# A new order table for a one-core adaLN block: attention tiles spread, w_sp blocks moved behind the stages' own transposes, x added by TensorE in five tiles

## The chip, the cores and the metric

The kernel runs on one core of one Trainium2 chip. The metric is the device time of one execution in microseconds (us), from the first to the last instruction and what lies around them. The kernel before has a median of 252.75 us over three runs (252.35, 252.75 and 254.44). A change of 1% is 2.5 us.

## What is computed

A block of a transformer with S = 2048 rows x, D = 448, 16 heads of width 28 (all in bfloat16). The reference, cut to what matters:

```
h = layernorm(x) * (1 + ca) + sa          # ca, sa, ... from silu(c) @ w_mod
q, k, v = h @ wqkv                        # 16 heads of 28
phi(t)  = [softmax(t @ w_phi), softmax(-t @ w_phi)]
o = (phi(q) @ (phi(k)^T v)) / (phi(q) . sum phi(k))
x = x + ga * (o @ wo)
h = layernorm(x) * (1 + cb) + sb
z = gelu(h @ w_in);  z1, z2 = halves of 896
g = w_sp @ layernorm(z2) + b_sp           # w_sp is 2048 x 2048: over the rows
out = x + gb * ((z1 * g) @ w_out)
```

## The kernel before, in words

The work is cut into 16 row tiles of 128 (numbers 0 to 15). All steps are emitted by one loop in `fast_path`, which reads a table of words, `ORDER`: `kM:12@A1` calls step `kM` for tile 12 with PSUM slot A1, `nA:8/V` calls `nA` for tile 8 on VectorE. An engine executes its instructions in the order of the words, so the table is the schedule. The letters behind a slash are engines: V is VectorE (DVE), S is ScalarE (ACT), G is GpSimd (POOL), Y is SyncE's DMA queue (SP). The slots behind @ are PSUM buffers: A0, A1, A2 of two banks, B0, B1 of one bank. A step that takes a slot waits until the readers of the slot's last contents are done.

The stages, by the words and the lines of the kernel before:

- **The ramp**: loads, weights folded with w_phi and the modulation, the first four tiles transposed by TensorE.
- **Keys and values**: `l1a` normalises a row tile on POOL (L824), `T1:a,b` has the SP queue transpose tiles a to b-1 into hT (L829), `kM` and `vM` are four matmuls each (L847, L855), `kE` and `kF` the exponentials on ACT (L850), `kS`, `kR`, `kP` the softmax sums and products (L861, L865, L868), `kA` adds a tile into phi(k)^T v (L878). `qM:n` makes features of 512 rows of q (L902, eight matmuls), `qE` and `qF` its two exponentials on ACT (L907).
- **Attention**: for each tile `nM` (L930, eight small matmuls into a slot A), `nX` (ACT, L938), `nC` and `nS` (DVE, L941 to L947; `nS` serves two tiles), `nT` (DVE, L950, the last reader of the slot), `nA` (DVE or POOL, L956), `T2` (SP transposes the result, L829), then `wM` or `wN`: four matmuls with wo (L966). In `wN` a fifth matmul with the identity adds x on TensorE (L964) and ACT copies the sum out with `wR:i/S` (L971). With `wM`, DVE adds x in `wR:i/V` (L973). Seven tiles go by `wN`: 0, 1, 2, 3, 4, 10, 11.
- **The second layernorm and the wide layer**: `wQ` (square and sum), `l2R`, `l2r`, `l2a` normalise tile i again, `T3:a,b` transposes it into hT over SP (L1004), `zM` is eight matmuls for z2 (L1010, slot A), `zG` its gelu on ACT (L1014), `zQ`, `zR`, `zW`, `zN` its layernorm. `yM:st,fc` is four matmuls for z1 (L1039), which need the four tiles 4st to 4st+3, `yG` its gelu on ACT (L1042). `SHw` and `SCw` fold the modulation into w_in (L740, L753 to L757), `csB`, `ccB` are its columns (L721).
- **The mixing by w_sp**: `W:t,u` (L1047) has the SP queue load and transpose one of 32 blocks (128 x 1024) of w_sp. `W:0` goes to a buffer of its own (f_wsp), `W:1` and `W:2` into the two halves of f_Eq, once `nM` has read tiles 0 to 7 or 8 to 15, `W:3` into hT, once all `zM` and `yM` are done. `gM` (L1106) and `P` (L1085) are the matmuls over w_sp, in a scheme with seven products for eight; `tT`, `sS` make their sums, `d` and `x` (L1094, L1101) read out; `oM` (L1120), `oE`, `oD` make and store the output.

SP's queue holds, besides the loads, all of T1, T2, T3 and W in the order of the words: one that waits holds up all behind it. The word `dm:9,3` issues nine small matmuls on zeros into a free corner of tile 3's slot (L935); they compute nothing.

Of the kernel before, what the change touches and what calls it, by code (L numbers as in the profile page):

```python
# [476 lines left out]
CB = HP * DH  # L477
TCHF = 512
SUM_MAX = 4.0e12

# [747 lines left out]
```

## Time and profile before

| What | Value |
|---|---|
| median of three runs | 252.75 us |
| the profiled execution | 253.16 us |
| its span, first to last instruction | 251.3 us |
| PE busy | 241.7 us (96%), 1550 matmuls |
| DVE, ACT, POOL busy | 186.2, 105.9, 119.1 us |
| DMA, 68208 packets | 25.23 MB |
| chain that ended last | PE 77%, DVE 11%, DMA 4%, POOL 3% |

Stage by stage, from the stretches of the trace: keys and values lie at about 21.5 to 54.1 us of the span, attention with the start of the wide layer at 54.1 to 105, the rest of the wide layer to 139.4, the mixing to the end. A row of the time line reads: start in us, length in us, engine, line, operation, out<-in, shapes, count, and in brackets how long the engine stood idle before it and what ended that. Rows of matmuls overlap: a row's length holds the time in which its last result drains, so the distance of two starts tells what a group costs, not its length.

### The profile page before, as it was taken

The numbers are of one execution on the slowest core, as the hardware profiler recorded it, in microseconds if no ns is written. First come the engines' busy times: TensorE is split into PE (matmuls) and PEld (weight loads), VectorE is DVE, ScalarE is ACT, GpSimd is POOL, SyncE is SP. The second block draws the span as 40 slices with busy tenths as digits, with TensorE's granted clock in tenths as the row PEclk, the third lists the DMA queues.
The fourth block names the chain that finished last, engine by engine and source line by source line (L and its number), as shares of the span: only waits on it lengthen the run. The fifth ranks groups of instructions, "written<-read, shape, count | busy, mean of one in ns | idle before, by whom it ended". The sixth has DMA issues, their size and how long they took to land.

```text
span 251.3 us, 4227 instructions
## 1 busy us (share of the span) xinstructions
PE 241.7 (96%) x1550; PEld 127.1 (51%) x1550; DVE 186.2 (74%) x378; ACT 105.9 (42%) x219; POOL 119.1 (47%) x161
## 2 busy tenths in 40 slices
PE   8999998999989799999999999999999999999993
PEld 5865555576546454444444444444444444444451
DVE  4799999777999968874548999599976436644552
ACT  2498977735879658896897300000000000000000
POOL 3749997503568663486834064101119511034530
PEclk9999999999999999999999999999999999999999
DMA  7987569951588849789691977000001000101022
GB/s 181 275 231 173 97 144 200 233 141 21 103 164 113 158 85 183 122 146 221 121 179 28 172 133 77 0 0 0 3 0 37 0 3 1 55 0 37 21 92 68
DMA packets 68208, 25.23 MB, mean 100 GB/s; under 512 B 58129, under 2 KB 67602, under 8 KB 68178
## 3 DMA queue, kind: packets, MB, share of 16 engines
q1 hardware_dynamic: 64848, 20.78, 42.5%
q10 hardware_dynamic: 3330, 4.09, 5.9%
q8 instruction: 14, 0.23, 0.4%
q14 instruction: 16, 0.13, 0.2%
HBM read 8.87 MB, written 1.84 MB: 43 GB/s over the span
## 4 chain that ended last, share of the span: by engine, by line
PE 77%; DVE 11%; DMA 4%; POOL 3%; issue 2%; ACT 1%; POOLq 0%; DVEq 0%
PE g_ps L1085 29%; PE z_ps L1039 10%; PE z_ps L1010 9%; PE o_ps L1120 8%; PE g_ps L1106 5%; DMA f_hT<-f_xpad 4%; PE x_ps L966 3%; PE warm_ps L686 3%; DVE f_st L813 3%; PE q_ps L902 2%; PE v_ps L855 2%; DVE f_ar L950 2%; PE kvacc L878 2%; DVE f_ksum L861 2%; PE num L930 2%
## 5 line engine op out<-in xcount | busy, mean ns | idle before, releaser
L1094 DVE TENSOR_TENSOR f_zb<-g_ps,f_zb 128x512 f32<-128x512 f32 (+1 forms) x31 | 20.3, 669 | 17.5 <-PE g_ps L1085 17.1
L1085 PEld LDWEIGHTS <-f_z2n 128*128 128x128 bf16 x192 | 18.8, 98 | 22.5
L1101 POOL TENSOR_TENSOR f_z1T<-f_zb,f_z1T 128x512 bf16<-128x512 f32 (+1 forms) x11 | 11.9, 1102 | 35.0 <-DVE f_zb L1094 35.0
L1039 PE MATMUL z_ps<-f_hT,f_ar 112*128 112x512 bf16 x112 | 26.3, 379 | 1.3 <-DMA f_hT<-f_xpad 1.3
L1010 PE MATMUL z_ps<-f_ar,f_hT 112*128 112x448 bf16 (+1 forms) x128 | 26.5, 352 | 0.0
L1120 PE MATMUL o_ps<-f_wout,f_z1T 128*128 128x448 bf16 x112 | 22.5, 352 | 0.0
L1085 PE MATMUL g_ps<-f_ar 128*128 128x512 bf16 x96 | 22.2, 379 | 0.0
L1042 ACT ACTIVATE f_z1T<-z_ps,f_zb 128x512 bf16<-128x512 f32 x28 | 18.4, 683 | 6.7 <-PE z_ps L1039 6.7
L1101 POOL TENSOR_TENSOR f_z1T<-f_Sx,f_z1T 128x512 bf16<-128x512 f32 x6 | 7.1, 1182 | 27.2 <-DVE f_Sx L1094 27.2
L907 ACT ACTIVATE f_Eq<-q_ps 112x1024 bf16<-112x1024 f32 x16 | 16.1, 1036 | 6.5 <-PE q_ps L902 6.5
L1010 PEld LDWEIGHTS <-f_hT 112*128 112x128 bf16 (+1 forms) x128 | 12.2, 97 | 11.7 <-DMA f_hT<-f_xpad 0.3
L1039 PEld LDWEIGHTS <-f_ar 112*128 112x128 bf16 x112 | 10.9, 97 | 14.2 <-issue 1.8
L861 DVE TENSOR_REDUCE f_ksum<-f_E 128x32 f32<-128x896 bf16 x16 | 16.7, 1056 | 1.4 <-ACT f_E L850 1.4
L950 DVE TENSOR_TENSOR f_ar<-num,f_w 128x896 bf16<-128x896 f32 x16 | 16.9, 1084 | 0.4
L1014 ACT ACTIVATE f_zb<-z_ps 128x896 bf16<-128x896 f32 x16 | 14.6, 915 | 5.6 <-PE z_ps L1010 4.4
L850 ACT ACTIVATE f_E<-k_ps 128x448 bf16<-128x448 f32 x32 | 16.0, 556 | 1.7 <-PE k_ps L847 1.6
L1085 PE MATMUL g_ps<-f_Eq,f_z2n 128*128 128x512 bf16 x72 | 16.7, 379 | 0.0
L1120 PEld LDWEIGHTS <-f_z1T 128*128 128x128 bf16 x112 | 11.0, 98 | 10.7
L1123 DVE TENSOR_TENSOR f_xpad<-o_ps,f_x 128x448 bf16<-128x448 f32 x16 | 9.9, 621 | 8.0 <-PE o_ps L1120 7.9
L847 PE MATMUL k_ps<-f_Wk,f_hT 113*128 113x448 bf16 (+1 forms) x64 | 14.6, 352 | 0.8 <-DMA f_hT<-f_xpad 0.8
L902 PE MATMUL q_ps<-f_hT,f_Wq 113*128 113x512 bf16 (+1 forms) x64 | 15.0, 379 | 0.1
L1085 PEld LDWEIGHTS <-f_ar 128*128 128x128 bf16 x96 | 9.4, 98 | 11.2
(207 smaller groups left out, 483.1 us busy)
## 6 DMA issues: line engine op xcount, KB each, us to landing
out_dram<-f_xpad SPq DMA_DIRECT2D x16, 112.0 KB, 1.7
f_ar<-in_B_w_in_dram ACTq DMA_DIRECT2D x2, 784.0 KB, 5.3
f_wm<-in_w_mod_dram SPq DMA_DIRECT2D x3, 406.0 KB, 5.8
f_x<-in_A_x_dram SPq DMA_DIRECT2D x2, 448.0 KB, 8.7
f_wmg<-in_w_mod_dram ACTq DMA_DIRECT2D x2, 392.0 KB, 4.2
f_wout<-in_B_w_out_dram SPq DMA_DIRECT2D x1, 784.0 KB, 5.3
f_bsp<-in_B_b_sp_dram SPq DMA_DIRECT2D x1, 512.0 KB, 4.3
f_x<-in_A_x_dram ACTq DMA_DIRECT2D x1, 448.0 KB, 6.3
```

The costliest lines, as they stand in the source:

```text
L850: nc.scalar.activation(out=Er[i % NR][:, s, :], in_=ps["k" + str(i)][:, 0, 0:D], func=ACT.Exp, scale=1.0 - 2.0 * s)
L861: nc.vector.tensor_reduce(out=ksum[:, i], in_=Er[i % NR][:].rearrange("p s (c f h) -> p (s c) h f", c=4, h=HP), axis=AX.X, op=ALU.add)
L902: nc.tensor.matmul(t[:, u, :], lhsT=Wq[0:KR[m], m, cc * CB:cc * CB + P], rhs=hT[0:KR[m], 4 * st:4 * st + 4, m, :], start=(m == 0), stop=(m ...
L907: nc.scalar.activation(out=Eq[st // 2][0:CB, 2 * c2:2 * c2 + 2, s, (st % 2) * 512:(st % 2 + 1) * 512], in_=ps["q" + str(n)][0:CB, :, :], f ...
L950: nc.vector.tensor_tensor(out=tr[i % 2][:], in0=numv(i)[:, :, :, 0:DH], in1=wr[i // 2 % 2][:, i % 2].unsqueeze(3).to_broadcast([P, 2, H, D ...
L1010: nc.tensor.matmul(t[:, hf, 0:D], lhsT=hT[0:KR[m], i, m, :], rhs=win_s[0:KR[m], m, FH + hf * D:FH + (hf + 1) * D], start=(m == 0), stop=(m ...
L1039: nc.tensor.matmul(t[:, 0, :], lhsT=win_s[0:CB, m, fc * P:(fc + 1) * P], rhs=hT[0:CB, 4 * st:4 * st + 4, m, :], start=(m == 0), stop=(m == ...
L1042: nc.scalar.activation(out=stage_b()["z1T"][:, fc, st * 512:(st + 1) * 512], in_=ps["y%d_%d" % (st, fc)][:, 0, :], func=ACT.Gelu_apprx_tan ...
L1085: nc.tensor.matmul(g, lhsT=sta[:, m, :], rhs=mov[:, m, :], start=(m == 0 and i in (1, 6, 7)), stop=(m == 7), skip_group_check=True)
L1094: nc.vector.tensor_tensor(out=o, in0=x, in1=y, op=ALU.add)
L1101: eng.tensor_tensor(out=z, in0=T[r][:, c0:c1], in1=z, op=ALU.mult)
L1120: nc.tensor.matmul(ps["o" + str(t)][:, 0, 0:D], lhsT=later["z1T"][:, FO[n], t * P:(t + 1) * P], rhs=wout_s[:, FO[n], :], start=(n == 0), s ...
```

## The change

The table is replaced by another with the same steps (894 words for 895). All words up to `gr:1` (21.5 us into the span) stay, apart from one slot of dummy matmuls. Behind them nearly every word has another place, some have another engine or slot. The number of instructions changes in two points. `dm` and its word go (nine matmuls). And one step `wM:i/E` replaces `wM` and `wN`: with S it adds x on TensorE, with V on DVE; now five tiles (0, 1, 2, 3, 5) go by S and eleven by V, instead of seven and nine.

The code, besides the table:

```diff
-    def dm(n, i):
-        for _ in range(n):
-            nc.tensor.matmul(ps["n" + str(i)][:, 1, 480:512], lhsT=zero[:, 0:P], rhs=zero[:, 0:32], start=True, stop=True)
-
...
-        "nM": nM, "nX": nX, "nC": nC, "nS": nS, "nT": nT, "nA": nA, "T2": T2, "wM": lambda i, slot: wM(i, slot, False), "wN": lambda i, slot: wM(i, slot, True),
+        "nM": nM, "nX": nX, "nC": nC, "nS": nS, "nT": nT, "nA": nA, "T2": T2, "wM": lambda i, slot, eng: wM(i, slot, eng is nc.scalar),
```

Four lines of the new table, the start of attention and the first tiles of the wide layer (the old table is one line of 6,700 characters):

```diff
+nX:0 nM:1@A0 nX:1 ld:win1/Y ccB@B0 csB@B1 nC:0 qF:3 nC:1 nS:0 nT:0 nA:0/V qM:4@A2 qM:5@A1 qF:4 nT:1 qE:4 nA:1/G nM:2@A0 nX:2 T2:0,1 wos:1/V esB ecB nM:3@A2
+nX:3 nC:2 FB@B1 wM:0/S@B0 nC:3 nS:1 qE:5 FBc/S qF:5 wR:0/S SHw:3@B1 SCw:0,3/S T2:1,2 nM:5@A1 nT:2 nX:5 nM:4@A0 nX:4 nT:3 nC:5 nC:4 nA:3/V nS:2 nT:5 wM:1/S@B0
+nA:2/G nT:4 wR:1/S T2:2,4 SHw:2@B1 wQ:0/S qM:6@A2 wQ:1/V nM:6@A1 SCw:0,0/S SCw:0,2/S qE:6 SCw:2,1/G nM:7@A0 nA:5/V wM:2/S@B1 nX:7 nA:4/V nC:7 wM:3/S@B0
+nX:6 SCw:3,1/G qF:6 wR:2/S T2:4,6 wQ:2/S wR:3/S nC:6 nS:3 nT:7 qM:7@A2 wQ:3/S nT:6 l2R:0,2/G qE:7 nA:6/V l2r:0,2 l2a:0/G nA:7/G nM:9@A0 nM:8@A1 nX:9 T3:0,1
```

**SP's queue in attention.** Before, from the first T2 (f_ar<-f_ar is T2, f_hT<-f_xpad is T3, anything from in_B_w_sp_dram a W block):

```order
L829 DMA_TRANSPOSE f_ar<-f_ar 128x4x128 x2
L1047 DMA_TRANSPOSE f_wsp_85<-in_B_w_sp_dram 128x8x128
L829 DMA_TRANSPOSE f_ar<-f_ar 128x8x128
L1047 DMA_TRANSPOSE f_wsp_85<-in_B_w_sp_dram 128x8x128
L1047 DMA_TRANSPOSE f_Eq<-in_B_w_sp_dram 128x8x128
L829 DMA_TRANSPOSE f_ar<-f_ar 128x8x128
L1047 DMA_TRANSPOSE f_wsp_85<-in_B_w_sp_dram 128x8x128
L1004 DMA_TRANSPOSE f_hT<-f_xpad 128x4x128
L829 DMA_TRANSPOSE f_ar<-f_ar 128x8x128
L1004 DMA_TRANSPOSE f_hT<-f_xpad 128x4x128
L1004 DMA_TRANSPOSE f_hT<-f_xpad 128x8x128
L1047 DMA_TRANSPOSE f_Eq<-in_B_w_sp_dram 128x8x128
```

The change, from the first T2 (its lines are numbered 38 or 42 higher):

```order
L871 DMA_TRANSPOSE f_ar<-f_ar 128x4x128 x2
L871 DMA_TRANSPOSE f_ar<-f_ar 128x8x128 x2
L1042 DMA_TRANSPOSE f_hT<-f_xpad 128x4x128
L871 DMA_TRANSPOSE f_ar<-f_ar 128x8x128
L1042 DMA_TRANSPOSE f_hT<-f_xpad 128x4x128
L1042 DMA_TRANSPOSE f_hT<-f_xpad 128x8x128
L871 DMA_TRANSPOSE f_ar<-f_ar 128x8x128
L1042 DMA_TRANSPOSE f_hT<-f_xpad 128x8x128
L1085 DMA_TRANSPOSE f_Eq<-in_B_w_sp_dram 128x8x128 x2
```

Before, a W block stands behind almost every transpose of the stage, from T2:1,2 on. Now ten transposes (to T3:4,6) stand with none between, and the first W blocks behind them.

**PE at qM:4.** Before, the matmuls of csB and ccB (cf_ps), then SHw:2 (sh_ps), then the first of qM:4 (q_ps):

```order
L721 MATMUL cf_ps<-f_scol,f_wm_119 128x1
L740 LDWEIGHTS f_Gb
L740 MATMUL sh_ps<-f_ar,f_Gb 128x448
...
L902 LDWEIGHTS f_Wq
L902 MATMUL q_ps<-f_hT,f_Wq 128x512
```

The change:

```order
L763 LDWEIGHTS f_wm_119
L763 MATMUL cf_ps<-f_scol,f_wm_119 128x1
L944 LDWEIGHTS f_Wq
L944 MATMUL q_ps<-f_hT,f_Wq 128x512
...
L972 MATMUL num<-f_ar,f_Eq 128x120
```

The four matmuls of SHw:2 no longer stand between the columns and qM:4, which takes slot A2 from qM:3; they stand behind wM:1 now.

**PE at the last attention tiles.** Before, zM:4 (z2_ps_1488, slot A1), nM:15, then nM:14 (num_1519, slot A1 again), then zM:5:

```order
L1010 MATMUL z2_ps_1488<-f_ar_76,f_hT_75 128x448
...
L930 MATMUL num_1503<-f_ar_76,f_Eq_107 128x120
...
L930 MATMUL num_1519<-f_ar_76,f_Eq_107 128x120
...
L1010 MATMUL z2_ps_1532<-f_ar_76,f_hT_75 128x448
```

The change, from zM:4 (slot A1) over two yM to nM:15 (num_1504, slot A1), nM:14 and zM:5:

```order
L1048 MATMUL z2_ps_1474<-f_ar_76,f_hT_75 128x448
...
L1077 MATMUL z1_ps_1486<-f_hT_75,f_ar_76 128x512
...
L1077 MATMUL z1_ps_1498<-f_hT_75,f_ar_76 128x512
...
L972 MATMUL num_1504<-f_ar_76,f_Eq_107 128x120
...
L972 MATMUL num_1515<-f_ar_76,f_Eq_107 128x120
...
L1048 MATMUL z2_ps_1524<-f_ar_76,f_hT_75 128x448
```

Between zM:4 and the next user of its slot stood one nM; now two yM stand there.

44 lines of the change are left out of this document (41 added, 3 removed).

## The prediction

> **What bounds the kernel now.** I read the page's busy shares first, then TensorE's time line, then what stands around each of its pauses.
>
> ```profile
> span 251.3 us, 4227 instructions
> PE 241.7 (96%) x1550; PEld 127.1 (51%) x1550; DVE 186.2 (74%) x378; ACT 105.9 (42%) x219; POOL 119.1 (47%) x161
> PEclk9999999999999999999999999999999999999999
> ```
>
> PE is the bound, at full granted clock in all 40 slices. A new order can win only the pauses of PE and the matmuls that go. In TensorE's time line between 40 and 97 us:
>
> ```profile
> 40.60 0.93 PE L855 MATMUL v_ps<-f_wv,f_hT 113*128 113x448 bf16 x4
> 42.30 0.93 PE L847 MATMUL k_ps<-f_Wk,f_hT 113*128 113x448 bf16 x4 [0.77 <-DMA f_hT<-f_xpad]
> ...
> 64.22 0.92 PE L740 MATMUL sh_ps<-f_ar,f_Gb 112*128 112x448 bf16 x4
> 65.30 1.00 PE L930 MATMUL num<-f_ar,f_Eq 112*128 112x120 bf16 x16 [0.16 <-DVE f_ar L950]
> ...
> 67.09 0.38 PE L935 MATMUL num<-f_zero 128*128 128x32 bf16 x9
> 67.53 1.90 PE L902 MATMUL q_ps<-f_hT,f_Wq 113*128 113x512 bf16 x8
> 70.03 0.59 PE L930 MATMUL num<-f_ar,f_Eq 112*128 112x120 bf16 x8 [0.61 <-DVE f_ar L950]
> 71.03 0.59 PE L930 MATMUL num<-f_ar,f_Eq 112*128 112x120 bf16 x8 [0.40 <-DVE f_ar L950]
> 71.46 0.35 PE L964 MATMUL x_ps<-f_x,f_ident 128*128 128x448 bf16 x1
> 71.65 0.92 PE L966 MATMUL x_ps<-f_ar 112*128 112x448 bf16 x4
> ...
> 82.28 0.92 PE L966 MATMUL x_ps<-f_ar 112*128 112x448 bf16 x4
> 84.51 1.02 PE L1039 MATMUL z_ps<-f_hT,f_ar 112*128 112x512 bf16 x4 [1.31 <-DMA f_hT<-f_xpad]
> 85.37 0.58 PE L930 MATMUL num<-f_ar,f_Eq 112*128 112x120 bf16 x8
> ...
> 88.92 0.58 PE L930 MATMUL num<-f_ar,f_Eq 112*128 112x120 bf16 x8
> ...
> 91.84 1.69 PE L1010 MATMUL z_ps<-f_ar,f_hT 113*128 113x448 bf16 x8
> 93.37 0.58 PE L930 MATMUL num<-f_ar,f_Eq 112*128 112x120 bf16 x8
> 94.63 0.58 PE L930 MATMUL num<-f_ar,f_Eq 112*128 112x120 bf16 x8 [0.68 <-ACT f_zb L1014]
> ```
>
> Starts give the cost of a group: a `zM`, eight matmuls of 448 columns, 1.53 us (91.84 to 93.37), so four of them 0.76; a `yM` 0.86 (84.51 to 85.37); an `nM` 0.43 (71.03 to 71.46). Eight q matmuls take 1.73 (sixteen in 3.64 with the last one's drain, further down). A pause is what lies between two starts beyond that: 0.94 us before `kM:12` (41.36 to 42.30), 0.32 before `nM:4`, 0.77 and 0.58 before `nM:7` and `nM:6`, 1.47 before `yM:0,0`, 0.84 before `nM:14`. Together **4.92 us**, besides some 0.3 in crumbs. Two come from DMA, three from `nT` on DVE, one from `zG` on ACT. From 97 us to the last matmul PE pauses nowhere longer than a tenth.
>
> **The change part by part. What goes:** the nine matmuls of `dm` cost 0.44 us (67.09 to 67.53). Two identity matmuls go, 0.19 each (71.46 to 71.65). That is **0.82 us**, surely on the path, as PE is. The two tiles cost DVE an addition in place of ACT's copy, with other work of PE beside it.
>
> **The w_sp blocks and the transposes.** The two DMA pauses, by the rows of these transposes alone (`T1:12,14`, `T3:2,4`), and of all T3:
>
> ```profile
> DMA to landing us min/median/max: 5.1/5.1/5.1
> ...
> DMA to landing us min/median/max: 4.9/4.9/4.9
> ...
> DMA to landing us min/median/max: 2.6/3.5/4.9
> ```
>
> ```profile
> 79.53 1.23 SPq L1004 DMA_TRANSPOSE f_hT<-f_xpad  x1
> 80.87 2.15 SPq L1047 DMA_TRANSPOSE f_Eq<-in_B_w_sp_dram  x1
> ...
> 102.89 5.39 SPq L1047 DMA_TRANSPOSE f_Eq<-in_B_w_sp_dram  x4
> ```
>
> The transpose issued at 79.53 lands at 84.4, with a W block of 256 KB issued right behind it. In the new order two more transposes stand behind it and no W. At the median, 3.5, it would land at 83.0, when PE came (82.28 + 0.76 = 83.04). So 1.47 becomes 0; bounds 0 and 1.47. For `kM:12` the order on PE alone nearly suffices: one more group of 0.76 stands ahead of it, so PE comes at 42.1. Its transpose was issued 5.1 before 42.3, at 37.2, behind POOL's normalisations, of which one less and one small pair more stand ahead of it now; w_mod's late load, which went with it, stands earlier. Issued at 37.2 again, it lands between 39.8 and 42.3. I take 0, bounds 0 and 0.2.
>
> What stands late next are the W blocks: 21 behind the last T3, for 14 before. The first consumer is `gM:0`, which needs `W:0,0`, the fifth behind it. At 1.35 us per issue (5.39 for four) it issues 5.4 us behind that T3's issue and lands, if as slowly as the slowest row above (4.9), at 10.3. PE works 8 `yM` and 3 `zM`, 11.5 us, between the first consumer of that T3, which lands some 2.1 us behind its issue, and `gM:0`, so 13.6. Margin 3 us; cost 0, bounds 0 and 1.
>
> **The last tiles spread.** `nM:14` waited for `zG:4` because one `nM` of 0.43 stood between two users of slot A1. ACT's rows show what slot reuse costs:
>
> ```profile
> 86.22 0.96 ACT L978 ACTIVATE f_ar<-f_zb 128x896 bf16<-128x896 bf16 x1
> ...
> 87.88 0.90 ACT L1014 ACTIVATE f_zb<-z_ps 128x896 bf16<-128x896 f32 x1
> ```
>
> A gelu (the second row, `zG:2`) takes 0.9 and starts some 0.2 behind its matmuls; a square of the same width (`zQ`, the first) takes 0.96. With the 1.53 us of `zM:3` between, `nM:12` started at 88.92, 0.14 behind that gelu's end and no more than a tenth behind the matmuls. The new table leaves 1.5 to 2.4 at all such places (here two `yM`, 1.73). So 0.84 goes. But where ACT has another piece ahead of the gelu, 1.5 doesn't suffice. By the table that is so three times: `zM:2` waits for `zG:1`, behind a scaling of w_in (about 0.25); `nM:12` for `zG:3`, with `zG:2` ahead (0.35); `yM:1,3` for `zG:5`, behind a `zQ` (0.2). Together **0.8**, bounds 0 and 4.7 (ten such places, 0.47 each, with a `zQ` of 0.95 ahead: 0.2 + 0.92 + 0.95 less 1.6).
>
> **New waits in attention.** `qM:4` takes slot A2 from `qM:3`:
>
> ```profile
> 54.08 1.90 PE L902 MATMUL q_ps<-f_hT,f_Wq 113*128 113x512 bf16 x8
> ...
> 57.46 0.93 PE L740 MATMUL sh_ps<-f_ar,f_Gb 112*128 112x448 bf16 x4
> 58.23 3.64 PE L902 MATMUL q_ps<-f_hT,f_Wq 113*128 113x512 bf16 x16
> ```
>
> ```profile
> 56.01 1.02 ACT L907 ACTIVATE f_Eq<-q_ps 112x1024 bf16<-112x1024 f32 x1 [2.79 <-PE q_ps L902]
> 56.93 0.27 ACT L938 COPY f_Sx<-num 128x32 f32<-128x32 f32 x2
> 57.07 1.05 ACT L907 ACTIVATE f_Eq<-q_ps 112x1024 bf16<-112x1024 f32 x1
> ```
>
> The second exponential ends at 58.12, and `qM:4` started at 58.23, right behind the sh_ps group that filled the time. That group has moved, ACT's order here has not. So PE would come at 57.46 and wait **0.8**; bounds 0 and 0.8. Behind it wait `qM:5` and `nM:2` on PE, which were due to wait for `nT:1` anyway.
>
> At `nM:6`, `nM:7` the chain is DVE's:
>
> ```profile
> 64.16 2.09 DVE L950 TENSOR_TENSOR f_ar<-num,f_w 128x896 bf16<-128x896 f32 x2
> 66.28 0.39 DVE L956 TENSOR_TENSOR f_ar<-f_ar 128x448 bf16<-128x448 bf16 x1
> 66.59 0.35 DVE L941 TENSOR_TENSOR f_cr<-num,f_Sx 128x32 f32<-128x32 f32 x2
> 66.97 0.62 DVE L945 TENSOR_TENSOR f_dn<-f_cr 128x32 f32<-128x32 f32 x1
> ...
> 72.10 0.19 DVE L945 TENSOR_TENSOR f_dn<-f_cr 128x32 f32<-128x32 f32 x1
> ```
>
> ```profile
> 66.35 2.19 POOL L755 TENSOR_SCALAR f_ar<-f_ar,f_cb 112x896 bf16<-112x896 bf16 x2
> ```
>
> From the end of `nM:4`, ACT's scaling and copies take 0.6, `nC` 0.3, `nA:3` 0.35, `nS` 0.85, each `nT` 1.05 and a little: 3.2 to the first `nT`, 4.25 to the second. PE has `wM:1` with x (0.95), SHw:2 (0.76), `qM:6` (1.73), 3.44, then `nM:6` 0.43. So `nM:6` doesn't wait and `nM:7` waits 0.4. With POOL's scaling of w_in beside it, as here, `nS` takes 0.8 longer (0.62 for 0.19 in its first row, the same in its last), and both waits come to 1.2. The new table keeps that POOL work next to `nS:2`. I take **0.8**.
>
> [...]
>
> `nM:8` waits for the second `nT` of its pair in the same way: 0.95 + 0.95 + 1.73 + 0.43 = 4.06 against a chain of 4.35, **0.3**, bounds 0 and 0.8. Without the pause at `kM:12`, `kA:15` comes earlier and would meet `kP:15` on DVE about **0.15** too early, bounds 0 and 0.3. The other moved steps lie beside PE's work: the loads of w_in and w_mod that pass to SP's queue stand behind the last T1, which needs nothing of theirs, and well ahead of their use.
>
> **The sum.** Pauses 4.92 to 0.8 + 0.8 + 0.8 + 0.3 + 0.15 = 2.85, crumbs 0.3 in both: 2.07 less. With 0.82 of removed work, 2.9 us. The profiled execution took 253.16 (span 251.3), so 250.3; it lay 0.4 above the median of 252.75, so I predict **249.9 us**.
>
> **Rivals.**
>
> *DVE and ACT chains take it all (0.27).* The transposes are in time, but PE comes earlier to the same chains: 0.8 at `qM:4`, 1.2 at `nM:7`, 0.8 at `nM:8`, 0.3 at `kA:15`, 1.5 at the gelus, 4.6 in all. Only 0.3 + 0.82 remain, 1.1 us: 251.6. For it: DVE is named in three of the six pauses, and the spacing is hardly wider there. Against it: the wider spacing at the slots.
>
> *All covers hold (0.10).* No new pause but crumbs: 4.92 + 0.82 = 5.7, 247.0. For it speak pauses of 0.1 wherever 1.5 us lay between. Against it the two exponentials at `qM:4`.
>
> *ACT's queue becomes the bound (0.10), slower.* Between 77 and 105 us ten steps of PE reuse a slot 1.5 to 1.75 us after the last user and wait for ACT. If a square of 0.95 always stands ahead, 4.7 comes for my 0.8, 3.9 more: 253.8; with a second square ahead at two of the ten, 1.9 on top: 255.7. It is slower than before from 0.37 us at each of the ten places on. For it: eleven `zQ` are ACT's, for ten. Against it: ACT is busy 42%, and waits for PE itself (2.79 us in a row above).
>
> *The clock drops (0.03), slower.* Without `dm` PE sits idle some 1.2 us together round `nM:7`. If the granted clock fell to half over 4 us of work, 4 us come on top: 253.9. In this trace a pause of 1.47 us didn't lower it. [...]
>
> **How the numbers follow.** My forecast has 0.50, with its own range 248.9 to 250.9. A change of 1%, 2.5 us, is about what a measurement of this kernel can tell; the line lies at 250.2. Of the forecast some 0.40 lies beyond it, with 0.10 of the covers that hold: faster 0.50. Within 1%: 0.10 of the forecast, 0.27, and half of ACT's 0.10 by its lower price, with rounding 0.42. Slower 0.08. The range is 247.9 to 252.9: it leaves out most of the case in which all holds, and the two slower ones.
>
> **What would show it.** Right: no pause on PE before `kM:12` and `yM:0,0`; `T3:2,4` landing in about 3.5; a pause of 0.8 before the third q group, ended by ACT's exponential; pauses at `nM:7` and `nM:8` ended by `nT`; none before `gM`. Wrong: a DMA at the head of a pause over 0.5 us between 55 and 140 us; a slice of granted clock under 9; pauses ended by `zG` of over 2 us together; no pause at `qM:4`.

## The result and the profile after

Twenty executions of the changed kernel took 250.94 us at the median (250.53 to 252.68), beside 253.15 for the kernel before on the same chip (20 executions, 251.72 to 254.48). The ratio is 0.992, with a 95% interval of 0.990 to 0.994: faster by 0.8%, 2.0 us (2.2 between the medians). That is clear of the noise, but inside the 1% that the prediction counts as no change. The forecast was 249.9. The profiled execution took 250.92. Of all executions behind this document one, of `after_tb`, took 365.98 us beside 249 to 252 of its others; it is left out.

The page of the changed kernel: its span, the busy shares, and the granted clock in 40 slices.

```profile
span 248.9 us, 4213 instructions
PE 240.5 (97%) x1539; PEld 126.7 (51%) x1539; DVE 184.2 (74%) x364; ACT 106.8 (43%) x219; POOL 123.2 (50%) x178
PEclk9999999999999999999999999999999999999998
```

PE is the bound as before: 1.2 us less busy, with the 11 matmuls fewer (9 of `dm`, 2 with the identity), and 2.4 us less span. The 8 in the last slice of the clock lies behind PE's last matmul, which ends at 244.6. Where its pauses went is seen from its busy time by stage. The columns are the stretch, its length, and then the busy time of PE with its instructions, of PEld, DVE, ACT and POOL, the granted clock, and DMA's share and GB/s. First the kernel before:

```profile
20.00:55.00 35.00, 34.23 (x273) 20.33 (x272) 31.53 (x59) 26.71 (x51) 25.37 (x24) 1.00 0.79 174
55.00:80.00 25.00, 23.77 (x242) 14.38 (x241) 21.32 (x52) 18.77 (x43) 14.32 (x23) 1.00 0.50 95
80.00:100.00 20.00, 18.01 (x120) 9.78 (x119) 16.77 (x46) 14.02 (x37) 11.79 (x21) 1.00 0.80 136
...
140.00:160.00 20.00, 20.00 (x95) 9.10 (x93) 19.55 (x22) 2.03 (x4) 7.85 (x3) 1.00 0.71 111
```

and the changed one in the same stretches:

```profile
20.00:55.00 35.00, 35.00 (x277) 20.80 (x276) 31.90 (x60) 27.11 (x51) 25.16 (x26) 1.00 0.80 170
55.00:80.00 25.00, 24.28 (x245) 15.09 (x244) 21.22 (x54) 21.09 (x51) 13.91 (x24) 1.00 0.42 68
80.00:100.00 20.00, 19.12 (x121) 10.11 (x120) 16.03 (x41) 18.14 (x41) 13.79 (x34) 1.00 0.75 141
...
140.00:160.00 20.00, 18.98 (x89) 8.36 (x87) 19.61 (x18) 0.00 (x0) 6.05 (x4) 1.00 1.00 159
```

Length less busy is PE's idle time: 0.77 to 0 in the first stretch, 1.23 to 0.72 in the second, 1.99 to 0.88 in the third. In the last, where the kernel before had none, there is now 1.02. TensorE's time line of the changed kernel shows each place:

```profile
41.85 0.58 PE L920 MATMUL kvacc<-f_vaug,f_phik 128*128 128x116 bf16 x8
42.27 0.92 PE L889 MATMUL k_ps<-f_Wk,f_hT 113*128 113x448 bf16 x4
...
55.79 0.94 PE L763 MATMUL cf_ps<-f_scol,f_wm 112*128 112x1 bf16 x32
57.31 3.63 PE L944 MATMUL q_ps<-f_hT,f_Wq 113*128 113x512 bf16 x16 [0.58 <-ACT f_Eq L949]
...
64.89 0.35 PE L1002 MATMUL x_ps<-f_x,f_ident 128*128 128x448 bf16 x1
65.38 0.93 PE L1004 MATMUL x_ps<-f_ar 112*128 112x448 bf16 x4
...
66.91 1.90 PE L944 MATMUL q_ps<-f_hT,f_Wq 113*128 113x512 bf16 x8
68.64 1.00 PE L972 MATMUL num<-f_ar,f_Eq 112*128 112x120 bf16 x16
...
80.31 0.92 PE L1004 MATMUL x_ps<-f_ar 112*128 112x448 bf16 x4
82.10 1.04 PE L1077 MATMUL z_ps<-f_hT,f_ar 112*128 112x512 bf16 x4 [0.88 <-DMA f_hT<-f_xpad]
...
146.11 3.63 PE L1123 MATMUL g_ps<-f_ar 128*128 128x512 bf16 x16
150.70 1.89 PE L1123 MATMUL g_ps<-f_wsp,f_z2n 128*128 128x512 bf16 x8 [0.96 <-DVE f_zb L1132]
```

Read as before, starts beyond what the group ahead costs: no pause at `kM:12` (42.27 follows an eight-matmul `kA` of 0.42). 0.72 us before `qM:4` (57.31, due 0.80 behind 55.79). 0.30 inside `wM:1`, between the matmul that adds x and the four that need `T2:1,2` (64.89 to 65.38, for 0.19). None at `nM:6` (68.64, 1.73 behind 66.91). 1.03 before `yM:0,0` (82.10, due 81.07). 1.13 before `P:0,0,2` (150.70; sixteen of these matmuls cost 3.46, so due 149.57), and 0.22 before `P:0,1,6` at 146.11. Nowhere else is there one of over 0.15 us. Sum 3.4, for 4.92 before: 1.5 less, and with the 0.82 of removed work 2.3, as the span has it.

Three of the five were not forecast at all, and one was to be gone: `yM:0,0` still waits for `T3:2,4`, which landed 4.61 us after its issue without a W block behind it. These were what the experiments had to explain.

### The profile page after: what moved, and what is told of

It is laid out like the page before. It is cut to its first block, busy times and chain, and to the rows that moved or that the text cites. A ratio compares the mean times of both kernels' runs of the same rounds, so it can differ in the third digit from the quotient of the medians.

```text
span 248.9 us, 4213 instructions
## 1 busy us (share of the span) xinstructions
PE 240.5 (97%) x1539; PEld 126.7 (51%) x1539; DVE 184.2 (74%) x364; ACT 106.8 (43%) x219; POOL 123.2 (50%) x178
## 4 chain that ended last, share of the span: by engine, by line
PE 76%; DVE 5%; ACT 5%; POOL 4%; issue 4%; DMA 4%; DVEq 0%; POOLq 0%
PE g_ps L1123 26%; PE o_ps L1158 9%; PE z_ps L1048 7%; PE z_ps L1077 6%; PE k_ps L889 5%; PE v_ps L897 5%; PE x_ps L1004 3%; PE q_ps L944 3%; PE g_ps L1144 3%; PE kvacc L920 3%; PE warm_ps L728 3%; DMA f_hT<-f_xpad 2%; DVE f_ar L1108 2%; DMA f_ar<-f_ar 2%; ACT f_ar L1016 2%
## 5 line engine op out<-in xcount | busy, mean ns | idle before, releaser
L1139 POOL TENSOR_TENSOR f_z1T<-f_Sx,f_z1T 128x512 bf16<-128x512 f32 x6 | 8.0, 1335 | 33.5 <-DVE f_Sx L1132 33.5
```

Of the source, the lines that this page charges most:

```text
L1139: eng.tensor_tensor(out=z, in0=T[r][:, c0:c1], in1=z, op=ALU.mult)
```

## The experiments

Each kernel was timed against the kernel before on its chip. Words of the order are named as above. Two things were first seen in the trace of the changed kernel. The DMA view of the two microseconds round the late transpose, the kernel before and then the changed one (the first row is the busy share in 40 slices of the stretch, 80.27 to 82.37 and 79.30 to 81.20; then the queue, kind: packets, MB, share):

```profile
DMA  0900000025999999999999999000000101000000
...
q8 instruction: 1, 0.02, 4.6%
```

```profile
DMA  9999999999999900000000000100110000000000
...
q8 instruction: 1, 0.02, 3.5%
```

In both a single packet of 16384 B of an instruction queue starts (80.37 and 79.44). Behind it the 256-byte packets of the transpose under way, 80 of them in a tenth of a microsecond, all but stop for over a microsecond: in the first view from 81.5 to its end, in the second from 79.95 on. In the list of packets some twenty took up to 1.5 us each (1.49 and 1.54 at the most), where others take 0.02. The packet comes when PE has started 728 matmuls before and 730 in the changed kernel. The next ones follow there at 854, 977, 1100 and 1224, in the kernel before at 111 to 139 from one to the next, some 126 in the mean of both. By this count the author took it for PE's own instructions. This gave the fetch theory (the packet makes the transpose late), against the forecast's (the W block behind). It can be tested without touching the order: fewer or more matmuls in the warm-up move the packet to another place of the work (80.37 to 82.42 in `before_f15`, 79.44 to 81.05 in `after_f10`).

The second thing is on DVE, the rows of the changed kernel:

```profile
138.71 2.61 DVE L1101 TENSOR_TENSOR f_z2n<-f_z2n 128x1024 bf16<-128x1024 bf16 x1
141.25 4.20 DVE L1108 TENSOR_TENSOR f_ar<-f_ar,f_wsp 128x4096 bf16<-128x4096 bf16 x1
```

and beside them on POOL:

```profile
138.21 2.57 POOL L1101 TENSOR_TENSOR f_ar<-f_z2n,f_ar 128x1024 bf16<-128x1024 bf16 x1 [2.94 <-PE z_ps L1077]
140.86 2.45 POOL L1101 TENSOR_TENSOR f_xpad<-f_z2n,f_ar 128x1024 bf16<-128x1024 bf16 x1
```

`tT:3,0` takes 2.61 us and `sS:0,2` 4.20, where other instructions of their sizes take 0.69 and 2.29 (rows further down): 3.8 us more together, beside POOL's `tT:2,0` and `tT:4,0`. In the kernel before `tT:2,0` stood on DVE; the new order has moved it to POOL, a word that the prediction passed over.

**The kernel before, the packet moved** (`before_f15`): the same columns in 15 fewer matmuls. The second number of a `du` is its width; without one it is 256.

```diff
-du:2@A1 ... du:3@A0 ... du:14@A1 ... du:3@B0 ... du:8@B1 ... du:2@B1
+du:1,512@A1 ... du:2,384@A0 ... du:7,512@A1 ... du:2,384@B0 ... du:4,512@B1 ... du:1,512@B1
```

> The kernel before with 15 fewer warm-up matmuls in its first 11 us, the rest wider, so that their columns are the same; the order of all engines stays. Fetch theory: in the trace of before a packet of 16384 B of an instruction queue starts at 39.21 and at 80.37 us, when PE stands at its 350th and 728th matmul, and the packets of the transposes that are under way stall behind it (one of 256 B takes up to 2.2 and 1.5 us for 0.02); that, not the W block behind, is what T1:12,14 and T3:2,4 wait for. With 15 matmuls fewer ahead the same packets come when PE stands 15 matmuls further on, near 43 and 82.4 us, between transposes. T3:2,4 then lands about 3.3 us after its issue for 4.9, the pauses before kM:12 (0.94) and yM:0,0 (1.47) go, with W:1,3 still right behind T3:2,4: 2.2 to 2.4 us less than before, about 250.8. The forecast's theory (the W block behind slows it): nothing changes, 253.1 within 0.3, with T3:2,4 at 4.9 still.

Measured: 253.26 beside 252.99 us, ratio 1.001 (0.998 to 1.003). The gain did not come. TensorE's rows:

```profile
38.06 1.00 PE L920 MATMUL kvacc<-f_vaug,f_phik 128*128 128x116 bf16 x16 [0.17 <-DVE f_phik L910]
...
41.69 0.92 PE L897 MATMUL v_ps<-f_wv,f_hT 113*128 113x448 bf16 x4
42.45 0.73 PE L889 MATMUL k_ps<-f_Wk,f_hT 113*128 113x448 bf16 x3
...
84.53 1.02 PE L1081 MATMUL z_ps<-f_hT,f_ar 112*128 112x512 bf16 x4 [1.18 <-DMA f_hT<-f_xpad]
```

The pause before `kM:12` did go (42.45 is 0.76 behind 41.69), but four smaller ones of 0.1 to 0.3 ahead of it, the first for DVE's `kP`, add up to 0.85, and the place gives nothing: `kM:12` starts at 42.45 for 42.30, since other chains come nearly as late there as the DMA did. `yM:0,0` still waits. The packet had moved as told, to 82.42, with 728 matmuls started; but it caught the transpose's end. The landing of a transpose stands in the trace as 16 completions: ten came at 82.72 to 82.88, the other six at 84.38 to 84.48. The time and the landing (4.80) are those that the forecast's theory gave; the fetch theory's gain did not come. What keeps it open is that the six late completions came at the end of a stop that follows the packet (83.04 to 84.42).

**The kernel before, one W block moved** (`before_w`), from behind `T3:2,4` to behind `T2:8,10`:

```diff
-T3:2,4 wR:6/V W:1,3 ... yG:0,0 W:0,7
+T3:2,4 wR:6/V ... yG:0,0 W:0,7 W:1,3
```

> The kernel before with one W block moved: W:1,3 stands on SP behind W:0,7 and so behind T2:8,10, no longer right behind T3:2,4. The forecast's theory: T3:2,4 lands in about 3.5 us for 4.9 and the pause before yM:0,0 (1.47) goes: 251.7. Fetch theory: the instruction packet still starts at 80.4, T3:2,4 lands in 4.6 to 5.0 as before, the pause stays: 253.1 within 0.3.

Measured: 253.16 beside 252.99, ratio 1.001 (0.998 to 1.003). `T3:2,4` landed in 4.44, and the pause before `yM:0,0` is 0.97 for 1.47. A new one of 0.55 (at 117.58, for a later T3) takes that back, so the landing tells here, and not the time. The forecast's step, that the W block behind the transpose made it late, fails: without the block most of the delay stays.

**The changed kernel, the packet moved** (`after_f10`):

```diff
-du:14@A1 ... du:8@B1
+du:7,512@A1 ... du:5,400@B1
```

> The changed kernel with 10 fewer warm-up matmuls in its first 9 us, the rest wider; the order stays. Fetch theory: the instruction packets that started at 63.15 and 79.44 us, with PE at its 602nd and 730th matmul, come 10 matmuls of PE later, at about 64.4 and 82, after T2:1,2 and T3:2,4 have landed. T2:1,2 lands in about 3 us for 4.1, T3:2,4 in 3.3 for 4.6; the waits inside wM:1 (0.31) and before yM:0,0 (1.03) go: 1.3 less than the changed kernel, about 249.6. Rival (T3:2,4 is late by what stands around it on SP, a transpose on either side): it lands in 4.6 again and the time is that of the changed kernel, 250.9 within 0.3.

Measured: 250.53 beside 252.99, ratio 0.989 (0.985 to 0.992). `T3:2,4` lands in 3.06, `T2:1,2` in 2.41, and both pauses are gone. The packet came at 81.05, 0.45 us ahead of that landing and not behind it as told; the stop that follows it, from 82.11 on, falls on the next transpose. The time fell by 0.4 for 1.3. In its profile PE was 1.3 us late at 58 us already (58.62 for 57.31): the warm-up had taken longer there, of which more at the end; for the other five executions that is not shown.

**The changed kernel with `tT:2,0` on DVE** (`after_t`):

```diff
-sS:0,4,0,8/V P:0,1,1 P:0,1,6 d:0,1,1 tT:2,0/G tT:4,0/G
+sS:0,4,0,8/V tT:2,0/V P:0,1,1 P:0,1,6 d:0,1,1 tT:4,0/G
```

> The changed kernel with tT:2,0 back on DVE, behind sS:0,4, so that POOL's tT:2,0 and tT:4,0 no longer run beside sS:0,2 and tT:3,0. Port theory: in the trace of after sS:0,2 takes 4.20 us and tT:3,0 2.61 beside these two of POOL, for 2.29 and 0.69 elsewhere; so DVE came 3.8 us late to the additions for which P:0,0,2 waits. They now take 2.3 and 0.7, and the pauses of 0.22 before P:0,1,6 and 1.13 before P:0,0,2 go: 1.2 to 1.35 less, about 249.6. Order theory (the pause comes from sS:0,4 standing ahead of the additions in the new order): DVE has 0.7 more ahead of them, the pause stays at 1 or grows: 250.9 to 251.6.

Measured: 249.73 beside 252.99, ratio 0.987 (0.983 to 0.991); 1.2 us under the changed kernel's 250.94. DVE's rows, to be held against those above:

```profile
138.34 0.69 DVE L1101 TENSOR_TENSOR f_z2n<-f_z2n 128x1024 bf16<-128x1024 bf16 x1
138.94 2.29 DVE L1108 TENSOR_TENSOR f_ar<-f_ar,f_wsp 128x4096 bf16<-128x4096 bf16 x1
...
141.74 2.29 DVE L1108 TENSOR_TENSOR f_ar<-f_wsp,f_ar 128x4096 bf16<-128x4096 bf16 x1
...
145.80 1.29 DVE L1132 TENSOR_TENSOR f_zb<-g_ps,f_bsp 128x512 f32<-128x512 f32 x2 [1.17 <-PE g_ps L1123]
```

`tT:3,0` and `sS:0,2` have their old durations, and DVE now waits for PE at the additions (1.17) instead of PE for DVE. The port theory, that POOL's two instructions beside them held these two up by 3.8 us together, holds; the order theory falls. By what means POOL holds DVE up is not shown.

**The changed kernel once more** (`after_c`), unaltered:

> The changed kernel once more, unaltered, beside the next three on one chip, so that they can be compared with it as well as with the kernel before. All theories: about 2.0 us under before, with pauses of PE of 0.7 before qM:4, 0.8 to 1.1 before yM:0,0 and 1.3 together at P:0,1,6 and P:0,0,2, as in its first profile; only the warm-up of the first 6 us may differ by up to 1 us, since the matmuls' spacing there falls from 0.21 to 0.11 us at another moment in each execution.

Measured: 251.33 beside 253.03, ratio 0.993 (0.991 to 0.995); `T3:2,4` in 4.73, and the same pauses but for the one in `wM:1`, which is under 0.1. It is the base of the next two.

**Both edits together** (`after_tf`), the diffs of `after_f10` and `after_t`:

> The changed kernel with both edits: 10 fewer, wider warm-up matmuls, and tT:2,0 on DVE. Fetch and port theories together: T2:1,2 lands in 2.4 and T3:2,4 in 3.1 us, no pause before yM:0,0, none before P:0,0,2; 1.3 and 1.3 under the changed kernel, 2.6 together, about 248.3. If the two pauses have one slack behind them (a later wait takes what the first gives): only one of the two counts, about 249.6. If the wider warm-up matmuls cost what they did in the first look (PE was 1.3 us late at 58 us): about 249.5, with the pauses gone all the same.

Measured: 248.49 beside 253.03, ratio 0.981 (0.979 to 0.984): 2.8 us under `after_c`, for 2.6 expected. TensorE's rows at the two places, without a wait:

```profile
80.54 0.92 PE L1004 MATMUL x_ps<-f_ar 112*128 112x448 bf16 x4
81.30 1.03 PE L1077 MATMUL z_ps<-f_hT,f_ar 112*128 112x512 bf16 x4
...
145.33 3.62 PE L1123 MATMUL g_ps<-f_ar 128*128 128x512 bf16 x16
148.78 1.89 PE L1123 MATMUL g_ps<-f_wsp,f_z2n 128*128 128x512 bf16 x8
```

The two gains add up: the one later wait that is new, 0.25 in `zM:3` at 83.94 for an `nT` on DVE, takes little of them.

**And work put ahead of `qM:4`** (`after_tfq`):

```diff
-ccB@B0 csB@B1 nC:0 qF:3 nC:1 nS:0 ... wos:1/V esB ecB ... nC:2 FB@B1
+csB@B1 ccB@B0 esB nC:0 qF:3 nC:1 FB@B1 nS:0 ... wos:1/V ecB ... nC:2
```

> The one before with one edit more: FB, 0.70 us of PE that needs nothing of qM:3, stands ahead of qM:4, with its input esB first on DVE. The forecast's theory of qM:4 (PE waits 0.7 for ACT's second exponential since no other work stands ahead): the pause goes and nothing takes its place, 0.7 under after_tf, about 247.6. Cover theory: what FB gives ahead of qM:4 is missing behind nM:3, where PE then waits for T2:0,1 or for DVE's nT: 0.7 comes back before wM:0 or wM:1, and the time is that of after_tf within 0.3.

Measured: 248.24, ratio 0.981 (0.978 to 0.984), 0.25 under `after_tf`, which is less than these times can tell. In the rows the pause before `qM:4` is gone and a smaller one stands further on:

```profile
56.88 0.84 PE L788 MATMUL fb_ps<-f_Gb,f_ar 112*128 112x1 bf16 x28
57.59 3.63 PE L944 MATMUL q_ps<-f_hT,f_Wq 113*128 113x512 bf16 x16
...
62.12 0.92 PE L1004 MATMUL x_ps<-f_ar 112*128 112x448 bf16 x4
63.34 0.92 PE L782 MATMUL sh_ps<-f_ar,f_Gb 112*128 112x448 bf16 x4 [0.30 <-ACT f_zb L825]
```

FB's copy (`FBc`, on ACT) frees the slot that `SHw:3` takes, and it stands behind an exponential; PE waits there 0.46 (63.34, due 62.88). So the forecast's cause of the pause at `qM:4` is right. The cover theory is right in that over half of it comes back, but at another place and for another engine than it named.

**The kernel before with the W part alone, in two tries** (`before_wall`, `before_wall2`). The blocks stand much as in the changed order: none between T2:0,1 and T3:4,6, then two, one and one, and the rest behind T3:10,12 and the two T3 after it. The words of SP's queue alone, without those between:

```diff
-T3:2,4 W:1,3 T2:8,10 W:0,7 T3:4,6 T2:10,12 T3:6,8 W:2,3 W:0,5 W:2,5 T2:12,14 T2:14,16 W:2,4 W:1,1 W:2,2 W:2,7 T3:8,10
+T3:2,4 T2:8,10 T3:4,6 W:0,1 W:0,6 T2:10,12 T3:6,8 T2:12,14 W:1,0 T2:14,16 W:0,3 T3:8,10
```

> The kernel before with the part on the w_sp blocks alone: as in the changed order, the blocks that stood between the stages' transposes stand behind T3:4,6, T2:12,14, T2:14,16, T3:10,12, T3:12,14 and T3:14,16; all else is as before. The forecast's theory: T3:2,4 lands in about 3.5, its pause of 1.3 to 1.5 goes: about 251.7. Fetch theory: PE's place at the instruction packet near 80.4 us is the same, T3:2,4 lands in 4.4 to 5.0 and the pause is 0.8 to 1.4; the time is that of before within 0.4.

Measured: 260.45 beside 253.03, ratio 1.029 (1.026 to 1.031). That says nothing about the part, since the order that was written put `W:1,6` behind six blocks of the second half, and `gM:1` needs it:

```profile
144.57 5.30 PE L1148 MATMUL g_ps<-f_Eq,f_z2n 128*128 128x512 bf16 x16 [4.88 <-DMA f_Eq<-in_B_w_sp_dram]
```

It does show what the margin before `gM` is worth when it is used up, and that such a wait costs more than itself. The four microseconds behind it, in the columns of the stages above:

```profile
144.50:148.50 4.00, 3.93 (x11) 1.53 (x12) 3.80 (x3) 0.00 (x0) 0.00 (x0) 0.57 1.36 152
```

The granted clock is 0.57 there, and the first eight matmuls stand 0.43 us apart for 0.22. None of the pauses told of in the other runs, the longest 1.47, did that; the forecast's rival of a lower clock had 1.2 us together, and that a pause of such a length lowers it no run shows.

In the second try `W:1,6` stands ahead:

> The part on the w_sp blocks alone once more, in an order that gM:1 can live with: W:1,6, for which it waited 4.9 us in the first try, stands ahead of the blocks of the second half, and only two blocks stand between T3:10,12 and T3:12,14. The forecast's theory: the pause before yM:0,0 goes (1.3 to 1.5 less): 251.6. Fetch theory with the share of W that the first try showed (T3:2,4 in 3.99 for 4.94, pause 0.4 for 1.3): 0.4 to 0.9 less, 252.2 to 252.6, unless a wait before gM takes it back.

Measured: 252.86 beside 253.19, ratio 0.998 (0.995 to 1.000). `T3:2,4` lands in 4.44 with no W behind it:

```profile
83.90 1.02 PE L1081 MATMUL z_ps<-f_hT,f_ar 112*128 112x512 bf16 x4 [0.83 <-DMA f_hT<-f_xpad]
```

The whole part on the blocks is worth some 0.3 us in the old order, if anything.

**The packet brought back** (`after_tb`): `after_tf` with ten matmuls of one column, the wide warm-up kept.

```diff
-du:5,400@B1
+du:5,400@B1 du:10,1@B1
```

> The version of 248.5 us (10 fewer, wider warm-up matmuls, tT:2,0 on DVE) with 10 matmuls of one column each added in the warm-up, so that the count of PE's instructions ahead of every stage is the changed kernel's again, while the wide warm-up stays. Fetch theory: the packet of 16384 B comes back to 79.5 us, on T3:2,4's packets; T3:2,4 lands in 4.5 to 4.8 for 3.04, T2:1,2 in 3.9 to 4.1 for 2.41, and PE pauses again 0.8 to 1.0 before yM:0,0 and 0.3 in wM:1: 1.1 to 1.3 more, 249.7, with 0.3 for the added matmuls 250.0. Rival (the wider warm-up matmuls, or the clock's rise, and not the count, moved the transposes out of harm): T3:2,4 lands in 3.0, no pause, 248.5 to 248.8.

Measured: 250.74 at the median of five executions (249.28 to 251.70) beside 253.19, ratio 0.989 (0.985 to 0.994). The profiled execution took 249.63, where 249.7 to 250.0 was expected; why the median lies higher is not shown. The packet is back at 79.44, with 730 matmuls started, and so is the wait:

```profile
80.31 0.92 PE L1004 MATMUL x_ps<-f_ar 112*128 112x448 bf16 x4
81.98 1.04 PE L1077 MATMUL z_ps<-f_hT,f_ar 112*128 112x512 bf16 x4 [0.75 <-DMA f_hT<-f_xpad]
```

`T3:2,4` lands in 4.48 and `T2:1,2` in 3.91, but `wM:1` does not wait this time. Ten one-column matmuls in the first ten microseconds cost PE 0.9 us (81.98, due 81.07) seventy microseconds later: the count decides, not the warm-up's form.

**A W block behind the transpose, twice.** `after_tfw` is `after_tf` with `W:1,1` moved up; `after_tgw` the same with 18 fewer warm-up matmuls for 10.

```diff
-T3:2,4 wR:4/V ... zQ:1/S W:1,1
+T3:2,4 W:1,1 wR:4/V ... zQ:1/S
```

> The version of 248.5 us with a W block (W:1,1) right behind T3:2,4 on SP, where before had one, and without a fetch on T3:2,4. The forecast's theory (a W block behind a transpose slows its landing): T3:2,4 lands in 4.5 or more for 3.04, and PE pauses about 1 before yM:0,0: 249.5. Fetch theory: it lands in 3.0 to 3.4, no pause; 248.5 within 0.3. By what the rows of before, of before with one block moved, and of before with all moved showed (its last increments 0.8 and 1.0 us behind the rest, then 0.2), a share of 0.5 is possible: it lands in 3.5 to 4 and PE waits up to 0.3.

Measured: 249.00 beside 253.19, ratio 0.983 (0.979 to 0.986). In its profile, which took 249.50, `T3:2,4` landed in 4.78: two of its 16 completions came at 80.64 and 80.80, the rest at 82.23 to 82.37, and the packet had started at 80.35.

```profile
82.42 1.04 PE L1077 MATMUL z_ps<-f_hT,f_ar 112*128 112x512 bf16 x4 [1.05 <-DMA f_hT<-f_xpad]
```

The landing and the pause are those of the forecast's theory; the next run takes the packet away and leaves the block.

> As the one before, with W:1,1 right behind T3:2,4, but 18 fewer warm-up matmuls for 10 (same columns), so that the packet of 16384 B, which started at 80.35, 0.3 us ahead of T3:2,4's first completions, comes about 1 us later, behind them. W theory (the block behind a transpose is enough to slow its landing): T3:2,4 lands in 4.5 or more again, PE pauses about 1 before yM:0,0; 249.0 to 249.5. Fetch theory (the block alone is harmless; it only kept the completions back until the packet's stall caught them): T3:2,4 lands in 3.0 to 3.4, no pause over 0.1 there; 248.4 to 248.7. If the packet meets T2:8,10 or T3:4,6 instead, yM:0,1 and yM:0,4 have more than 1 us in hand and nothing is to be seen on PE.

Measured: 248.30 beside 253.36, ratio 0.980 (0.977 to 0.983). The packet starts at 82.64, `T3:2,4` lands in 3.68, and PE all but goes through:

```profile
79.94 0.92 PE L1004 MATMUL x_ps<-f_ar 112*128 112x448 bf16 x4
80.82 1.04 PE L1077 MATMUL z_ps<-f_hT,f_ar 112*128 112x512 bf16 x4
```

A block behind costs the transpose 0.6 (3.68 for 3.04 to 3.06), which the slack of 0.5 nearly covers; with the packet on top it costs 1.7. At that place the two are needed together: in `after_tf` a packet 2.6 us behind the issue, without a block, cost the transpose nothing. All runs in one table, the packet counted from the issue of `T3:2,4`:

| kernel | packet, us behind the issue | W block behind | `T3:2,4` lands in |
|---|---|---|---|
| before | 0.8 | yes | 4.94 |
| before_w, before_wall, before_wall2 | 0.7, 1.1, 0.7 | no | 4.44, 3.99, 4.44 |
| before_f15 | 2.7 | yes | 4.80 |
| after, after_c, after_t, after_tb | 2.0 | no | 4.61, 4.73, 4.47, 4.48 |
| after_tfw | 2.8 | yes | 4.78 |
| after_f10, after_tf, after_tfq | 2.6 | no | 3.06, 3.04, 3.05 |
| after_tgw | 5.6 | yes | 3.68 |

The 4.94 of the kernel before holds one thing more. A second, shorter stop, from 83.79 to 84.42, stands ahead of its last seven completions (84.39 to 84.47), 0.6 us behind a packet of 8192 B of another instruction queue (83.16). So the 0.5 between `before` and `before_w` is not surely the block's, and its share rests on `after_tgw`, one profile. There, too, a stop stands ahead of the last four completions (0.4 us, from 80.37), with no instruction packet near.

## Why the prediction came out as it did

The time was inside the range and 1.0 us above the forecast; on the sum's own base, the span, 2.4 were won for 2.9, and the kernel before has a median of 253.15 on twenty executions for the 252.75 on three from which the forecast started. Faster by over 1%, which had the largest chance (0.50), did not come; within 1% (0.42) did. The size of the gain was about right, the places were only half right.

**Right.** The removed work, 0.82, is in the count of matmuls. `kM:12` has no pause: its transpose `T1:12,14` lands in 3.14 us (40.29), 2 us ahead of its use, and the packet now meets `T1:14,16`, which nobody awaits. `before_f15` adds that in the old order other waits come nearly as late at this place; the new one doesn't meet them. `qM:4` waits 0.72 for ACT's second exponential, forecast 0.8, and goes free when FB stands ahead of it. Before `gM` nothing waits; `before_wall` shows that the margin was no formality. `nM:14` no longer waits for `zG:4`.

**Wrong: `yM:0,0`, 1.47 to 0.** The failing step is that the transpose was slow because a W block was issued right behind it, so that it would land at the median of its kind. The block's share is some 0.6 (`after_tgw`); the greater part is the instruction packet, which stands in the changed kernel nearly at the same matmul (730 for 728), so that the transpose took 4.61 for the 3.5 of the forecast. The row that the prediction quoted (the slowest of the T3 had a W behind) fitted both, and the packets round the transpose were not looked at. The list of what would prove it wrong had this sign: a DMA at the head of a pause over 0.5 us between 55 and 140 us.

**Wrong: the new waits for ACT and DVE, 0.8 at the slots, 0.8 at `nM:6` and `nM:7`, 0.3 at `nM:8`, 0.15 at `kA:15`.** All are 0 to 0.15. At the slots ACT had been given the older gelu or square early enough. At `nM:7` half of the 0.8 was to come from POOL's scaling beside `nS:2`. POOL's row, and then DVE's: the sum in `nS:2`, and the two `nT` behind it:

```profile
66.99 2.01 POOL L797 TENSOR_SCALAR f_ar<-f_ar,f_cb 112x896 bf16<-112x896 bf16 x2 [1.62 <-PE sh_ps L782]
```

```profile
65.72 0.18 DVE L983 TENSOR_TENSOR f_dn<-f_cr 128x32 f32<-128x32 f32 x1
...
66.58 2.09 DVE L988 TENSOR_TENSOR f_ar<-num,f_w 128x896 bf16<-128x896 f32 x2
```

POOL's first word of that pair now waits for `SHw:2` on PE, 1.3 us behind `nS:2`, so the sum takes 0.18 and not 0.62. That wait could have been read from the order. From the end of `nM:4` (64.89, where `wM:1` starts) to that of the second `nT` (68.67) the chain took 3.8 us for the 4.25 of the sum. PE's work there is 3.87, and 4.17 with the pause in `wM:1`; in `after_tf`, without that pause, `nM:7` doesn't wait either.

**Not seen: 0.22 and 1.13 at `P:0,1,6` and `P:0,0,2`.** The prediction said that from 97 us on PE doesn't pause, and costed only W's arrival there. The word `tT:2,0` had gone from DVE to POOL, and the prediction itself had reckoned with POOL beside DVE at `nS` (0.62 for 0.19). `after_t` returns 1.2. Also not seen was the 0.30 in `wM:1`, again the packet (at 63.15, on `T2:1,2`, whose last two packets, of 4 B, came a microsecond behind the others).

So the forecast's losses of 2.05 that did not come stood against 2.7 that were not seen or not won (1.03, 0.30, 1.35): that the gain came so near 2.9 is luck, two errors of opposite sign.

**Open.** Why one such packet stops the others for a microsecond, no run here tells. Stops of 0.3 to 0.8 us, and in the changed kernel two of over one (1.3 from 98.58, 1.1 from 110.48), stand in the lists of packets with no instruction packet near; that the packet is the cause is shown for `T3:2,4` alone, by moving it. In `before_w` and `before_wall2` the last of the 16 completions came 1.0 us behind the other fifteen; that too stays without a cause. In `after_tfw` the profile shows one execution, and others of 248.8 to 249.1 may have missed the packet.

## What to carry to other kernels

When one transfer of a kind lands a microsecond late, look at all packets of that microsecond, those of the instruction queues too, before the neighbour on its own queue is blamed; and move the suspect without touching the order (here by some warm-up matmuls) to see whether the delay moves with it. A word that changes its engine is a change even where its place stays: list those first, and ask what runs beside it on the other engines at that moment (here two instructions of POOL, beside which two of DVE took 3.8 us more). A stall that is taken away shows the next chain, so a gain is only believed when the places ahead and behind have been read again.

## What the runs showed of the hardware

Packets of 16384 B of one instruction queue (q8) start about every 126 matmuls (in the kernels before and after 111 to 142 from one to the next, from the 350th to the 1492nd). Where one met `T3:2,4` in these two, the transpose's packets all but stopped for over a microsecond; the first slow ones started 0.84 and 0.32 us behind it (one of 256 B took up to 1.49 and 1.54 for 0.02). `T3:2,4`, two tiles, lands in 3.04 to 3.06 us undisturbed, 3.68 with a W block behind, 3.99 to 4.73 with such a packet on it, and 4.78 to 4.94 with both.

The warm-up's length differs between executions of the same instructions. The first 28 matmuls of the changed kernel, in its two profiles:

```profile
1.23 4.92 PE L728 MATMUL warm_ps<-f_zero 128*128 128x256 bf16 x28 [1.23 <-DVE f_zero L686]
```

```profile
1.23 5.38 PE L728 MATMUL warm_ps<-f_zero 128*128 128x256 bf16 x28 [1.23 <-DVE f_zero L686]
```

Their spacing falls from 0.21 to 0.11 us at one moment, behind the 16th in the first; in other profiles of 28 equal ones behind the 13th to the 21st. From `after_t`, behind the 13th, to `after_c`, behind the 21st, the start of `qM:4` moves from 57.17 to 57.70: 0.5 us, of the 2.1 by which executions of the changed kernel differ (250.53 to 252.68).
